# Attention, then four experts: the product of a first-batch pair in six parts, each behind a step's scores

## The chip, the cores and the metric

The kernel runs on one core of one Trainium2 chip. The metric is the device time of one execution in microseconds (us), lower is better: 772.12 us is the median of three runs of the kernel before (770.01 to 773.18).

## The reference

Two batches of eight heads, 768 tokens, 64 dimensions each. Each head's attention is masked by a hash: a query sees a key only where the signs of six projections agree. The attention output, 1536 rows of 512, then runs through four experts of one hidden layer (512 to 1024 to 512), weighted by row.

```python
q_bits = (np.einsum('bhsd,dk->bhsk', q, proj) > 0).astype(np.int64)
k_bits = (np.einsum('bhsd,dk->bhsk', k, proj) > 0).astype(np.int64)
...
mask = q_bucket[:, :, :, None] == k_bucket[:, :, None, :]
scores = scale * np.matmul(q, k.transpose(0, 1, 3, 2))
scores = np.where(mask, scores, -1000000000.0)
scores = scores - np.max(scores, axis=-1, keepdims=True)
attn = np.exp(scores)
attn = attn / (np.sum(attn, axis=-1, keepdims=True) + 1e-09)
return np.matmul(attn, v).astype(np.float32)
...
for e in range(E):
    h = np.maximum(x @ w1[e], 0.0)
    out += p[:, e:e + 1] * (h @ w2[e])
```

## The kernel before

The work comes in three stages. First the attention of batch 0 runs by itself. Then the experts work on batch 0 while the attention of batch 1 is fed in between their matmul groups at a set pace. Last the experts work on batch 1, with fewer products (`moe_fast`).

The attention advances in steps. Step i is query tile t = i mod 6 of head i div 6, so batch 0 has steps 0 to 47 and batch 1 steps 48 to 95; below, "scores 18" are those of step 18. The string `ORDER` says in which order a step's stages are issued, and each stage has a lag, the number of steps by which it trails the scores that it works on:

- S, `stage_s`: four matmuls on TensorE into a score tile `sps`, then a row minimum on VectorE (L368) into the tile `p`. `sps` has the PSUM tag `big`, of which there are two; `tps` and `hps`, used to prepare the next head, take the same two.
- E, `stage_e`: the exponential on ScalarE, one step behind. X, `stage_x`: a transpose on VectorE into `pt` (L415), two steps behind in batch 0, three in batch 1. `pt` has few buffers, so a head's first transpose waits for the product of an earlier pair.
- N, `stage_n`: the reciprocal of a head's row sums, stored to DRAM as `row`. R, `stage_r`: `row` read back from DRAM, spread over 64 partitions, into half of `rdb`.
- V, `stage_v`: the product of the probabilities of a pair of heads with `v` (tiles `tv`, output `pv`), 192 small matmuls in the program. Each of these is two weight loads and two matmuls in the trace, so a pair has 384 there. In batch 0 `pv` lies in four one-bank tiles; in batch 1 it takes both `big` tiles.
- U, `stage_u`: ScalarE copies `pv` out into `xf`, and SP issues the loads of the next pair's `v`. M, `stage_m`: GpSimd scales `xf` by `rdb` and splits it into two parts `xs` (three instructions for each half of the tokens, L465, L467, L470).
- P: one piece of the preparation of the next head (`prep_head`): six transposes `tps` at t = 0, a split on ScalarE and VectorE with copies on GpSimd (`q`, `q`, `k`), then six matmuls `hps` and a copy `ah`, signs on ScalarE, and at last the copies `al` (L332) and `k` on GpSimd. The next head's first scores read `al` and `k`.

A pair's last step is called its end: 11, 23, 35, 47 in batch 0. Before, V of the first three pairs comes in two halves of 96 matmuls, first thing in steps end+3 and end+4; the last pair's comes whole in step 50, and each pair of batch 1 has it whole in step end+4. U follows in step end+5 (51 for the last pair, end+4 in batch 1), M in the next two steps (51 for the last pair). Each engine does its instructions in the order in which they were issued, and so does each queue of DMA issues (SP's above all).

The expert weights are split into two parts on ScalarE and GpSimd (`w1lo`, `w2lo`, L571), the first expert's during the attention of batch 0. The first expert begins when both halves of the last pair are out (`done_b`): 12 matmuls of its first layer (L670 to L672, three for each pair of heads) for each of four blocks of the hidden layer. A group of matmuls of either layer is the unit between which the attention of batch 1 is fed.

Of the kernel before, what the change touches and what calls it, by code (L numbers as in the profile page):

```python
# [8 lines left out]
F32 = mybir.dt.float32  # L9
# [5 lines left out]
P = 128  # L15
# [6 lines left out]
LAG_N = 3  # L22
LAG_R = 4
LAG_X = (2, 3)
LAG_V = (3, 4)
V_PARTS = 2
PV_COST = 1950
# [11 lines left out]
ORDER = "VUXSRMENP"  # L39
# [5 lines left out]
def tile_lsh_attention__then__domain_moe(  # L45
# [24 lines left out]
    GN = S // G  # L70
    NBK = S // 32
# [133 lines left out]
    def load_v(b, h):  # L205
        t = ld.tile([P, QD, NT, D], F32, tag="tv", name="tv", bufs=2)
        for a in range(QD):
            nc.sync.dma_start(
                out=t[a * 32 : (a + 1) * 32], in_=v[b, h].rearrange("(r k c) d -> k r c d", r=QD, c=NT)
            )  # L210
        vvs[b, h] = t
# [179 lines left out]
    def stage_n(b, h):  # L391
# [6 lines left out]
    def stage_r(b, h):  # L398
        j, odd = divmod(h, 2)
        if not odd:  # L400
            rdbs[b, j] = xs.tile([P, S], F32, tag="rdb", name="rdb", bufs=1)
        row = rows.pop((b, h))
        nc.sync.dma_start(
            out=rdbs[b, j][odd * D : (odd + 1) * D], in_=row.rearrange("p t -> (p t)").partition_broadcast(D)
        )
# [11 lines left out]
    def parts_of(b, h):  # L417
        return 1 if b or h >= PB else V_PARTS

    def stage_v(b, j, part, n_parts):  # L420
        if part == 0:
# [4 lines left out]
        n = NBK // n_parts  # L426
        for k in range(part * n, (part + 1) * n):
# [13 lines left out]
    def stage_u(b, j):  # L441
        banks = pvs.pop((b, j))
        for i in range(2):
            vvs.pop((b, 2 * j + i))
            pts.pop((b, 2 * j + i))
            nxt = b * H + 2 * j + 2 + i
            if nxt < len(hseq):
                load_v(*hseq[nxt])
# [6 lines left out]
        for a in range(QD):  # L455
            nc.scalar.activation(xv[:, a], banks[a][:, : NT * 32].rearrange("p (t q) -> p t q", q=32), ACTF.Copy)

    def stage_m(b, h, g):
        j = h // 2
        sl = slice(g * GN, (g + 1) * GN)  # L460
        x = xraw[:, j, sl] if b else xf[j][:, sl]
        tg = NT // G
        rdb = rdbs[b, j].rearrange("d (p t) -> d t p", t=NT)[:, g * tg : (g + 1) * tg]
        x3 = x.rearrange("d (t p) -> d t p", t=tg)
# [8 lines left out]
        if (h, g) == (H - 1, G - 1):  # L473
            done_b[b] = True
# [3 lines left out]
    done_b = [False] * B  # L478

    def attention():  # L480
        n = len(seq)
        prep = [iter(())]

        def do(op, i):
            if op == "N":
                j = i - LAG_N
                if 0 <= j < n and j % NT == NT - 1:
                    stage_n(*seq[j][:2])
            elif op == "R":
                j = i - LAG_R  # L490
                if 0 <= j < n and j % NT == NT - 1:
                    stage_r(*seq[j][:2])
# [14 lines left out]
            elif op in "VUM":  # L507
                for back in range(min(LAG_V), max(LAG_V) + V_PARTS + 3):
                    j = i - back
                    if not 0 <= j < n or j % NT != NT - 1 or seq[j][1] % 2 == 0:  # L510
                        continue
                    b, h, _ = seq[j]
                    part, parts = back - LAG_V[b], parts_of(b, h)
                    if op == "V" and 0 <= part < parts:
                        stage_v(b, h // 2, part, parts)
                        return 2 * PV_COST * b
                    if op == "U" and part == (0 if b else parts):
                        stage_u(b, h // 2)
                    for g in range(G if op == "M" else 0):
                        if part == (parts if (b, h) == (0, H - 1) else (1 if b else 1 + parts) + g):  # L520
                            stage_m(b, h, g)
# [431 lines left out]
```

## Time and profile before

| | |
|---|---|
| time, median of three runs | 772.12 us (770.01 to 773.18) |
| the profiled execution: time, span | 772.6 us, 770.9 us |
| TensorE matmuls busy, share of the span | 720.2 us, 93% |
| VectorE busy | 473.2 us, 61% |
| ScalarE busy | 276.8 us, 36% |
| GpSimd (POOL) busy | 303.9 us, 39% |
| granted TensorE clock, mean | 0.947 |

The profile comes from one execution. "Busy" is time in which an engine has an instruction in work; for TensorE matmuls overlap, and their ends are modelled. PE is TensorE, DVE VectorE, ACT ScalarE, POOL GpSimd, SP the engine whose queue issues nearly all DMAs. [...]

### The profile page before, as it was taken

Reading aid. Unit: us, or ns where it says so; the run is one execution under the profiler, and the core shown is the slowest. Engines: PE = TensorE matmul, PEld = TensorE weight load, DVE = VectorE, ACT = ScalarE, POOL = GpSimd, SP = SyncE. Lnnn points to the kernel's source line nnn. Section 1 sums busy time; section 2 is a strip of 40 time slices with the busy share of each in tenths; the row PEclk is TensorE's granted clock in tenths of the full one; section 3 lists DMA queues with packets and bytes.
Section 4 is the critical chain, followed back from the end, with each engine's and each line's share of the span. In section 5 each row is a group of like instructions: output and inputs, shape, how many; then the busy total and the mean of one; then the engine's idle time right before and its main releaser. Section 6 shows DMA issues by size and latency. Waiting matters only on the chain.

```text
span 770.9 us, 14888 instructions
## 1 busy us (share of the span) xinstructions
PE 720.2 (93%) x6232; PEld 643.3 (83%) x6232; DVE 473.2 (61%) x766; ACT 276.8 (36%) x542; POOL 303.9 (39%) x279
## 2 busy tenths in 40 slices
PE   7888888939989998999899999999999999999998
PEld 5676676839879997899889898989989899899896
DVE  6857667415824781578168233488686686866853
ACT  5646555305303340243133111245343353343430
POOL 5265646132413542453242133375342342433420
PEclk9587887759999999999999999999999999999999
DMA  9335527160215331621422111214131212211202
GB/s 189 63 84 118 115 61 142 33 112 1 58 58 120 79 83 30 147 63 53 121 82 67 30 60 61 82 53 140 56 99 41 79 55 82 82 55 56 84 26 83
DMA packets 65555, 59.76 MB, mean 78 GB/s; under 512 B 38224, under 2 KB 46672, under 8 KB 65488
## 3 DMA queue, kind: packets, MB, share of 16 engines
q1 hardware_dynamic: 64464, 58.48, 30.0%
q8 instruction: 49, 0.80, 0.4%
q10 hardware_dynamic: 1024, 0.33, 0.2%
q14 instruction: 18, 0.15, 0.1%
HBM read 55.60 MB, written 3.19 MB: 76 GB/s over the span
## 4 chain that ended last, share of the span: by engine, by line
PE 87%; DVE 8%; issue 2%; DMA 2%; ACT 0%; POOL 0%; ACTq 0%; SPq 0%; POOLq 0%; DVEq 0%
PE mps L610 11%; PE mps L612 11%; PE mps L611 11%; PE pv L432 10%; PE mps L671 6%; PE mps L670 6%; PE mps L672 6%; PE sps L361 4%; DVE p L368 4%; PE sps L363 4%; DVE pt L415 3%; PE hps L316 3%; PE mps L825 2%; PE mps L821 2%; PE mps L824 2%
## 5 line engine op out<-in xcount | busy, mean ns | idle before, releaser
L610 PE MATMUL mps<-w2hi,hb 128*128 128x512 f32 (+1 forms) x388 | 150.8, 389 | 0.0
L612 PE MATMUL mps<-w2hi,hb 128*128 128x512 f32 (+1 forms) x388 | 150.6, 388 | 0.0
L611 PE MATMUL mps<-w2lo,hb 128*128 128x512 f32 (+1 forms) x388 | 150.4, 388 | 0.0
L384 ACT ACTIVATE p<-p,nb 128x768 f32<-128x768 f32 x96 | 89.8, 936 | 83.3 <-DVE p L368 82.9
L604 DVE SCALAR_TENSOR_TENSOR acc<-mps,pe,acc 128x512 f32<-128x512 f32 (+1 forms) x85 | 63.0, 742 | 86.3 <-PE mps L612 86.2
L368 DVE TENSOR_SCALAR_CACHE_REDUCE p<-sps 128x768 f32<-128x768 f32 x96 | 89.0, 927 | 43.5 <-PE sps L363 43.5
L676 ACT ACTIVATE hb<-mps 128x384 fp32r<-128x384 f32 x64 | 31.4, 490 | 200.8 <-PE mps L672 200.8
L670 PE MATMUL mps<-xs,w1hi 128*128 128x384 f32 x256 | 87.2, 341 | 12.9 <-POOL xs L467 12.3
L677 DVE SCALAR_TENSOR_TENSOR hb<-mps,hb 128x384 fp32r<-128x384 f32 x64 | 35.6, 556 | 95.6 <-ACT hb L676 95.4
L415 DVE STREAM_TRANSPOSE pt<-p 128x768 f32<-128x768 f32 x96 | 92.6, 965 | 0.0
L671 PE MATMUL mps<-xs,w1hi 128*128 128x384 f32 x256 | 87.0, 340 | 0.4 <-POOL xs L470 0.4
L672 PE MATMUL mps<-xs,w1lo 128*128 128x384 f32 x256 | 86.9, 339 | 0.0
L612 PEld LDWEIGHTS mps<-w2hi,hb 128*128 128x128 f32 x388 | 72.8, 188 | 16.1
L611 PEld LDWEIGHTS mps<-w2lo,hb 128*128 128x128 f32 x388 | 72.9, 188 | 14.0
L610 PEld LDWEIGHTS mps<-w2hi,hb 128*128 128x128 f32 x388 | 72.9, 188 | 13.8 <-issue 0.6
L432 PE MATMUL pv<-pt,tv 32*64 32x192 f32 x3072 | 74.5, 342 | 8.4 <-issue 8.4
L807 POOL TENSOR_TENSOR w2lo<-ws,w2hi 128x512 fp32r<-128x512 f32 x32 | 40.6, 1289 | 105.6 <-ACT w2hi L806 105.6
L571 POOL TENSOR_TENSOR w1lo<-ws,w1hi 128x512 fp32r<-128x512 f32 x32 | 41.3, 1291 | 101.7 <-DVE w1hi L579 87.0
L432 PEld LDWEIGHTS pv<-pt,tv 32*64 32x64 f32 x3072 | 66.0, 140 | 16.5 <-issue 14.8
L361 PE MATMUL sps<-ah,q 128*128 128x384 f32 x192 | 60.7, 401 | 17.8 <-DVE p L368 16.6
L571 POOL TENSOR_TENSOR w2lo<-ws,w2hi 128x512 fp32r<-128x512 f32 x32 | 41.3, 1293 | 61.1 <-issue 26.0
L361 PEld LDWEIGHTS sps<-ah,q 128*128 128x128 f32 x192 | 37.1, 216 | 33.5 <-DVE p L368 18.1
(127 smaller groups left out, 1264.2 us busy)
## 6 DMA issues: line engine op xcount, KB each, us to landing
ws<-in_moe_w_dram SPq DMA_DIRECT2D x64, 512.0 KB, 3.7
tv<-in_v_dram SPq DMA_DIRECT2D x64, 192.0 KB, 5.8
rdb<-row SPq DMA_DIRECT2D x16, 192.0 KB, 3.9
out_dram<-acc SPq DMA_DIRECT2D x11, 256.0 KB, 2.1
tqk<-in_q_dram SPq DMA_DIRECT2D x10, 192.0 KB, 6.0
tqk<-in_k_dram SPq DMA_DIRECT2D x10, 192.0 KB, 5.9
tqk<-in_q_dram SPq DMA_DIRECT2D x12, 96.0 KB, 2.9
tqk<-in_k_dram SPq DMA_DIRECT2D x10, 96.0 KB, 3.2
```

What stands on the lines that cost most here:

```text
L361: nc.tensor.matmul(ps[:, i, :NH], q1[:, sl], k1[:, i * NH : (i + 1) * NH], start=True, stop=False)
L368: nc.vector.tensor_scalar(out=two(pt), in0=ps[:, :, :NH], scalar1=MASKED, scalar2=MASKED, op0=ALU.min, op1=ALU.min, accum_out=nb,)
L384: nc.scalar.activation(pt, pt, ACTF.Exp, bias=nb, scale=-1.0, accum_out=den[:, t : t + 1])
L415: nc.vector.transpose(out=pts[b, h][:, :, t], in_=p.rearrange("p (k n) -> p k n", n=32))
L432: nc.tensor.matmul(pvs[b, j][a][i * D : (i + 1) * D, : NT * 32], vvs[b, 2 * j + i][rows, r, c], pts[b, 2 * j + i][rows, k].rearrange("p t ...
L571: nc.gpsimd.tensor_tensor(out=lo[:, c - 1], in0=st[c - 1], in1=hi[:, c - 1].bitcast(F32), op=ALU.subtract)
L610: nc.tensor.matmul(ps, hh[:, ts], w2hi[:, f, cs], start=n == 0, stop=False)
L611: nc.tensor.matmul(ps, hh[:, ts], w2lo[:, f, cs], start=False, stop=False)
L612: nc.tensor.matmul(ps, hl[:, ts], w2hi[:, f, cs], start=False, stop=n == FC - 1)
L670: nc.tensor.matmul(ps[:, :SB], w1hi[:, kk, fs], xhi[b, kk][:, sl], start=kk == 0, stop=False)
L671: nc.tensor.matmul(ps[:, :SB], w1hi[:, kk, fs], xlo[b, kk][:, sl], start=False, stop=False)
L672: nc.tensor.matmul(ps[:, :SB], w1lo[:, kk, fs], xhi[b, kk][:, sl], start=False, stop=kk == KD - 1)
```

## The change

A pair of batch 0 gets its product in six parts of 32 matmuls, in steps end+3 to end+8, each issued behind that step's scores; the last pair has two parts in each of the steps 50, 51 and 52. U comes a step after the last part (end+9, for the last pair 53), M in the two steps after (for the last pair 53 and 54). In batch 1 the product comes in three parts of 64 matmuls in step end+3, behind the scores, with a charge to the pace after each (the pace decides how many expert groups stand between two parts). The reciprocals N come ahead of the scores and a step earlier in batch 0; the rows R of both heads are read in step end+3, ahead of the scores and of v's loads. The `v` of pairs 1 and 3 of batch 0 is loaded into the memory of the output sums, so that a pair's `v` is loaded one pair earlier. The first expert begins its first half of the tokens when that half of the last pair is out (`done_g`), and its second half when the other is.

```diff
-LAG_N = 3
-LAG_R = 4
+LAG_N = (2, 3)
 LAG_X = (2, 3)
-LAG_V = (3, 4)
-V_PARTS = 2
-PV_COST = 1950
+V_AT = (3, 4, 5, 6, 7, 8)
+V_LAST = (3, 3, 4, 4, 5, 5)
+V_LATE = 3
+PV_COST = 3900
...
-ORDER = "VUXSRMENP"
+ORDER = "UXNRSVvwWMEP"
...
     def load_v(b, h):
-        t = ld.tile([P, QD, NT, D], F32, tag="tv", name="tv", bufs=2)
+        shape = [P, QD, NT, D]
+        if (b, h // 2) in ((0, 1), (0, 3)):
+            t = ap_.tile(shape, F32, tag=f"acc{h % 2}", name="tv")
+        else:
+            t = ld.tile(shape, F32, tag="tv", name="tv", bufs=2)
...
-    def stage_n(b, h):
+    def stage_n(b, h, t):
+        if t != NT - 1:
+            return
...
-    def stage_r(b, h):
-        j, odd = divmod(h, 2)
-        if not odd:
-            rdbs[b, j] = xs.tile([P, S], F32, tag="rdb", name="rdb", bufs=1)
-        row = rows.pop((b, h))
-        nc.sync.dma_start(
-            out=rdbs[b, j][odd * D : (odd + 1) * D], in_=row.rearrange("p t -> (p t)").partition_broadcast(D)
-        )
+    def stage_r(b, j):
+        rdbs[b, j] = xs.tile([P, S], F32, tag="rdb", name="rdb", bufs=1)
+        for i in range(2):
+            nc.sync.dma_start(
+                out=rdbs[b, j][i * D : (i + 1) * D],
+                in_=rows.pop((b, 2 * j + i)).rearrange("p t -> (p t)").partition_broadcast(D),
+            )
...
-    def parts_of(b, h):
-        return 1 if b or h >= PB else V_PARTS
-
-    def stage_v(b, j, part, n_parts):
-        if part == 0:
+    def stage_v(b, j, blocks):
+        if blocks.start == 0:
             if b:
                 pvs[b, j] = [x[:, i] for x in (big("pv"), big("pv")) for i in range(2)]
             else:
                 pvs[b, j] = [one("pv") for _ in range(QD)]
-        n = NBK // n_parts
-        for k in range(part * n, (part + 1) * n):
+        for k in blocks:
...
     def stage_u(b, j):
-        banks = pvs.pop((b, j))
-        for i in range(2):
-            vvs.pop((b, 2 * j + i))
-            pts.pop((b, 2 * j + i))
-            nxt = b * H + 2 * j + 2 + i
-            if nxt < len(hseq):
-                load_v(*hseq[nxt])
...
+        for a, bank in enumerate(pvs.pop((b, j))):
+            nc.scalar.activation(xv[:, a], bank[:, : NT * 32].rearrange("p (t q) -> p t q", q=32), ACTF.Copy)
+        for i in range(2):
+            vvs.pop((b, 2 * j + i))
+            pts.pop((b, 2 * j + i))
+            nxt = b * H + 2 * j + i + (2 if b else 4)
+            if nxt < len(hseq) and (b, j) != (0, H // 2 - 1):
+                load_v(*hseq[nxt])
...
+        if (b, j) == (0, H // 2 - 1):
+            done_g[g] = True
...
+    events = {}
+
+    def plan():
+        def at(step, op, f, *args):
+            events.setdefault((step, op), []).append((f, args))
+
+        for b in range(B):
+            for j in range(H // 2):
+                end = (b * H + 2 * j + 1) * NT + NT - 1
+                at(end + 3, "R", stage_r, b, j)
+                if b:
+                    steps, ops = (V_LATE,) * 3, "Vvw"
+                else:
+                    steps, ops = (V_LAST if j == H // 2 - 1 else V_AT), "VVVVVV"
+                n = NBK // len(steps)
+                for part, (step, op) in enumerate(zip(steps, ops)):
+                    at(end + step, op, stage_v, b, j, range(part * n, (part + 1) * n))
+                done = steps[-1] + (not b)
+                at(end + done, "W" if b else "U", stage_u, b, j)
+                for g in range(G):
+                    soon = (b, j) == (0, H // 2 - 1)
+                    at(end + done + (g if soon else 1 + g), "M", stage_m, b, j, g)
...
         def do(op, i):
             if op == "N":
-                j = i - LAG_N
-                if 0 <= j < n and j % NT == NT - 1:
-                    stage_n(*seq[j][:2])
-            elif op == "R":
-                j = i - LAG_R
-                if 0 <= j < n and j % NT == NT - 1:
-                    stage_r(*seq[j][:2])
+                for b, lag in enumerate(LAG_N):
+                    j = i - lag
+                    if 0 <= j < n and seq[j][0] == b:
+                        stage_n(*seq[j])
...
-            elif op in "VUM":
-                for back in range(min(LAG_V), max(LAG_V) + V_PARTS + 3):
-                    j = i - back
-                    if not 0 <= j < n or j % NT != NT - 1 or seq[j][1] % 2 == 0:
-                        continue
-                    b, h, _ = seq[j]
-                    part, parts = back - LAG_V[b], parts_of(b, h)
-                    if op == "V" and 0 <= part < parts:
-                        stage_v(b, h // 2, part, parts)
-                        return 2 * PV_COST * b
-                    if op == "U" and part == (0 if b else parts):
-                        stage_u(b, h // 2)
-                    for g in range(G if op == "M" else 0):
-                        if part == (parts if (b, h) == (0, H - 1) else (1 if b else 1 + parts) + g):
-                            stage_m(b, h, g)
+            elif op in "RVvwUWM":
+                c = None
+                for f, args in events.get((i, op), ()):
+                    f(*args)
+                    if op in "Vvw" and args[0]:
+                        c = 2 * PV_COST // 3
+                return c
...
-                    if (b, h, t) == (0, 0, 4):
-                        load_v(0, 1)
+                    if b == 0 and h < 2 and t in ((4,), (2, 4))[h]:
+                        load_v(0, (h + t) // 2 + 1 if h else 1)
...
-        for i in range(n + max(LAG_V) + 4):
+        for i in range(n + V_LATE + 2):
...
                 if u == 0:
-                    accs[b, tt] = ap_.tile([P, DM], F32, tag=f"acc{tt}", name="acc")
+                    if t == 0:
+                        group = ap_.tile([P, TS, DM], F32, tag=f"acc{s}", name="acc")
+                    accs[b, tt] = group[:, t]
...
+                while not done_g[s]:
+                    next(att)
...
-        while not done_b[0]:
+        while not done_g[0]:
...
-        n_att = H * (NT * 652 + 1632 + PV_COST) + (max(LAG_V) + 4) * DRAIN
+        n_att = H * (NT * 652 + 1632 + PV_COST) + (V_LATE + 2) * DRAIN
```

Three places show what this does to the engines' orders. The first is GpSimd around steps 18 to 24, in which the head with scores 24 to 29 is prepared; before, its `k` tile is called `k_762`.

```order
L465 TENSOR_TENSOR xf<-xf,rdb 128x384
L467 TENSOR_SCALAR xs_111<-xf 128x384
L470 TENSOR_TENSOR xs_111<-xf,xs_111 128x384
L571 TENSOR_TENSOR w1lo<-ws,w1hi 128x512
L220 TENSOR_SCALAR q_759<-ah 64x768 x2
L220 TENSOR_SCALAR k_762<-ah 64x768
L220 TENSOR_SCALAR ah<-al 64x768
L571 TENSOR_TENSOR w1lo<-ws,w1hi 128x512
L332 TENSOR_SCALAR al<-k_762,bit_mul 44x768
L220 TENSOR_SCALAR k_762<-al 12x768
```

After, the same head's tile is `k_719`. The six instructions of M of the first pair (`xf`, `xs_111`), which stood ahead of the preparation, now stand between its `ah` and its `al`, with a weight split among them.

```order
L225 TENSOR_SCALAR ah<-al 64x768
L464 TENSOR_TENSOR xf<-xf,rdb 128x384
L466 TENSOR_SCALAR xs_111<-xf 128x384
L469 TENSOR_TENSOR xs_111<-xf,xs_111 128x384
L582 TENSOR_TENSOR w1lo<-ws,w1hi 128x512
L464 TENSOR_TENSOR xf<-xf,rdb 128x384
L466 TENSOR_SCALAR xs_111<-xf 128x384
L469 TENSOR_TENSOR xs_111<-xf,xs_111 128x384
L337 TENSOR_SCALAR al<-k_719,bit_mul 44x768
L225 TENSOR_SCALAR k_719<-al 12x768
```

The second place is SP's queue at the end of batch 0. Before, the last pair's second row broadcast `rdb` stands behind the eight loads of `tv`, which are issued when the product is done.

```order
L396 DMA row<-rd 128x6
L403 DMA rdb<-row 64x768
L200 DMA tqk<-in_q_dram 128x6x64
L200 DMA tqk<-in_k_dram 128x6x64
L396 DMA row<-rd 128x6
L208 DMA tv<-in_v_dram 32x4x384 x8
L403 DMA rdb<-row 64x768
L191 DMA tqk<-in_q_dram 32x24x32 x2
```

After, both broadcasts of the last pair stand together with no `tv` load between them and their `row`; the `tv` loads (of batch 1's first pair) stand ahead of that and wait for the third pair only.

```order
L213 DMA tv<-in_v_dram 32x4x384 x8
L403 DMA row<-rd 128x6
L201 DMA tqk<-in_q_dram 128x6x64
L201 DMA tqk<-in_k_dram 128x6x64
L408 DMA rdb<-row 64x768 x2
L192 DMA tqk<-in_q_dram 32x24x32 x2
```

The third place is TensorE where batch 1's first pair has its product. Before, all 192 matmuls stand between groups of an expert (`mps`).

```order
L670 MATMUL mps<-xs_114,w1hi 128x384
L671 MATMUL mps<-xs_114,w1hi 128x384
L672 MATMUL mps<-xs_114,w1lo 128x384
L432 MATMUL pv<-pt,tv 64x192 x192
L670 MATMUL mps<-xs_111,w1hi 128x384
L671 MATMUL mps<-xs_111,w1hi 128x384
L672 MATMUL mps<-xs_111,w1lo 128x384
```

After, the first 64 stand right behind a step's scores, and 36 expert matmuls come before the next 64; the same rows stand for the other pairs but that one or four expert groups lie between scores and product.

```order
L621 MATMUL mps<-w2hi,hb 128x512
L622 MATMUL mps<-w2lo,hb 128x512
L623 MATMUL mps<-w2hi,hb 128x512
L366 MATMUL sps<-ah,q_2037 128x384 x2
L368 MATMUL sps<-k_2040,al 128x384 x2
L434 MATMUL pv<-pt,tv 64x192 x64
L621 MATMUL mps<-w2hi,hb 128x512
L622 MATMUL mps<-w2lo,hb 128x512
L623 MATMUL mps<-w2hi,hb 128x512
```

## Rows read from the trace of the kernel before

**Rows 1.** The page, part 2: the granted clock of TensorE by slices, in tenths.
```profile
PEclk9587887759999999999999999999999999999999
```

**Rows 2.** The waits of the whole span: sum in us, times, longest.
```profile
DVE p L368 <- PE sps L363: 43.5, 18, 10.4
```

**Rows 3.** Timeline 130 to 182 us: start, duration, engine, line, tiles [idle before <- releaser].
```profile
142.93 8.94 PE L432 MATMUL pv<-pt,tv 32*64 32x192 f32 x384
...
151.69 1.00 ACT L456 ACTIVATE xf<-pv 128x192 f32<-128x192 f32 x4 [6.37 <-PE pv L432]
...
154.35 4.04 SPq L208 DMA_DIRECT2D tv<-in_v_dram  x8
...
158.61 0.48 SPq L403 DMA_DIRECT2D rdb<-row  x1
...
165.50 1.18 POOL L465 TENSOR_TENSOR xf<-xf,rdb 128x384 f32<-128x384 f32 x1 [22.17 <-DMA rdb<-row]
...
168.42 0.69 PE L671 MATMUL mps<-xs,w1hi 128*128 128x384 f32 x1 [0.39 <-POOL xs L470]
...
174.02 0.52 PE L672 MATMUL mps<-xs,w1lo 128*128 128x384 f32 x1
...
175.22 0.34 PE L670 MATMUL mps<-xs,w1hi 128*128 128x384 f32 x1
```

**Rows 4.** Timeline 51 to 80 us: scores, a pair's first half, copies on POOL.
```profile
54.32 0.58 PE L361 MATMUL sps<-ah,q 128*128 128x384 f32 x2 [0.86 <-DVE p L368]
...
59.78 1.73 POOL L220 TENSOR_SCALAR q<-ah 64x768 fp32r<-64x768 f32 x2
...
68.18 0.58 PE L361 MATMUL sps<-ah,q 128*128 128x384 f32 x2 [0.87 <-DVE p L368]
...
72.56 5.68 PE L432 MATMUL pv<-pt,tv 32*64 32x192 f32 x192
```

**Rows 5.** Timeline 79 to 110 us: that pair's second half and the scores behind it.
```profile
80.12 4.16 PE L432 MATMUL pv<-pt,tv 32*64 32x192 f32 x192
...
84.21 0.62 PE L361 MATMUL sps<-ah,q 128*128 128x384 f32 x2
...
85.02 0.52 PE L361 MATMUL sps<-ah,q 128*128 128x384 f32 x2
...
88.08 0.58 PE L361 MATMUL sps<-ah,q 128*128 128x384 f32 x2 [0.87 <-DVE p L368]
```

**Rows 6.** Windows: length, busy us (instructions) of PE, PEld, DVE, ACT, POOL, clock, DMA.
```profile
54.00:68.00 14.00, 10.92 (x36) 8.60 (x36) 11.88 (x23) 8.57 (x16) 11.76 (x14) 0.63 0.80 145
```

**Rows 7.** Timeline 205 to 245 us: the product of the second batch's first pair.
```profile
217.69 2.86 PE L432 MATMUL pv<-pt,tv 32*64 32x192 f32 x128
...
221.61 2.86 PE L432 MATMUL pv<-pt,tv 32*64 32x192 f32 x128 [1.06 <-issue]
```

**Rows 8.** The waits of TensorE from 168 to 450 us.
```profile
PE pv L432 <- issue: 8.1, 7, 1.7
```

**Rows 9.** The page, part 5: groups of a step; busy us, mean ns | idle before.
```profile
L384 ACT ACTIVATE p<-p,nb 128x768 f32<-128x768 f32 x96 | 89.8, 936 | 83.3 <-DVE p L368 82.9
...
L368 DVE TENSOR_SCALAR_CACHE_REDUCE p<-sps 128x768 f32<-128x768 f32 x96 | 89.0, 927 | 43.5 <-PE sps L363 43.5
...
L415 DVE STREAM_TRANSPOSE pt<-p 128x768 f32<-128x768 f32 x96 | 92.6, 965 | 0.0
```

**Rows 10.** Groups on POOL by shape: busy us, mean ns | idle before.
```profile
L571 POOL TENSOR_TENSOR w1lo<-ws,w1hi 128x512 fp32r<-128x512 f32 x32 | 41.3, 1291 | 101.7 <-DVE w1hi L579 87.0 <-issue 7.6 <-DVE rd L394 5.7
...
L220 POOL TENSOR_SCALAR q<-ah 64x768 fp32r<-64x768 f32 x30 | 27.1, 903 | 62.1 <-ACT ah L229 60.9
...
L465 POOL TENSOR_TENSOR xf<-xf,rdb 128x384 f32<-128x384 f32 x8 | 9.6, 1200 | 30.1 <-DMA rdb<-row 24.2 <-DMA tv<-in_v_dram 4.5 <-ACT xf L456 1.4
L470 POOL TENSOR_TENSOR xs<-xf,xs 128x384 fp32r<-128x384 f32 x8 | 8.0, 1002 | 0.7
...
L467 POOL TENSOR_SCALAR xs<-xf 128x384 fp32r<-128x384 f32 x8 | 4.1, 511 | 0.7
```

More of the change, by code (lines that the diff above doesn't have):

```diff
@@ L70, in tile_lsh_attention__then__domain_moe @@
     GN = S // G
+    TG = NT // G
     NBK = S // 32
@@ L454, in stage_u, with stage_m @@
         xv = x.rearrange("p (t a q) -> p a t q", t=NT, q=32)
[L455 to L459, printed above, removed]
+        for a, bank in enumerate(pvs.pop((b, j))):
[6 more added lines that the diff above has]
+                load_v(*hseq[nxt])
+    def stage_m(b, j, g):
         sl = slice(g * GN, (g + 1) * GN)
         x = xraw[:, j, sl] if b else xf[j][:, sl]
-        tg = NT // G
-        rdb = rdbs[b, j].rearrange("d (p t) -> d t p", t=NT)[:, g * tg : (g + 1) * tg]
-        x3 = x.rearrange("d (t p) -> d t p", t=tg)
+        rdb = rdbs[b, j].rearrange("d (p t) -> d t p", t=NT)[:, g * TG : (g + 1) * TG]
+        x3 = x.rearrange("d (t p) -> d t p", t=TG)
         nc.gpsimd.tensor_tensor(out=x3, in0=x3, in1=rdb, op=ALU.mult)
@@ L472, in stage_m @@
             )
-        if (h, g) == (H - 1, G - 1):
-            done_b[b] = True
+        if (b, j) == (0, H // 2 - 1):
+            done_g[g] = True
     hseq = [(b, h) for b in range(B) for h in range(H)]
     seq = [(b, h, t) for b, h in hseq for t in range(NT)]
-    done_b = [False] * B
+    done_g = [False] * G
+    events = {}
[18 more added lines that the diff above has]
+                    at(end + done + (g if soon else 1 + g), "M", stage_m, b, j, g)
     def attention():
@@ L482, in attention @@
         prep = [iter(())]
+        plan()
         def do(op, i):
             if op == "N":
-                j = i - LAG_N
-                if 0 <= j < n and j % NT == NT - 1:
-                    stage_n(*seq[j][:2])
-            elif op == "R":
-                j = i - LAG_R
-                if 0 <= j < n and j % NT == NT - 1:
-                    stage_r(*seq[j][:2])
+                for b, lag in enumerate(LAG_N):
+                    j = i - lag
+                    if 0 <= j < n and seq[j][0] == b:
+                        stage_n(*seq[j])
             elif op == "X":
```

## The prediction

> **What bounds the kernel now.** I read the page first, for its clock row: TensorE has the full clock from about 175 us to the end, and less than that only ahead of it, in the attention of batch 0 and the handover to the experts [rows 1]. TensorE's waits say the same: behind the handover it waits almost only in the products of batch 1, 8.1 us [rows 8]. So there are three places with something to win or lose: the steps of batch 0, the handover, and the four products of batch 1. The rest is TensorE work that the change doesn't touch.
>
> In the steps of batch 0, VectorE paces. A step costs it a row minimum of 0.93 us and a transpose of 0.97 us [rows 9], a little overlapped; only while a half of a product stands in TensorE's queue ahead of the next scores does it wait: 43.5 us in 18 waits over the span [rows 2].
>
> At the handover the reader is to see one queue. The last product runs from 142.93 to 151.87 us and is copied out by 152.7. But the broadcast of the reciprocals leaves SP only at 158.61, behind eight loads of `tv` issued from 154.35 on, which wait for that product. GpSimd's scaling waits for it until 165.50, and the first expert's group, which needs it, ends at 169.1 (168.42 + 0.69) [rows 3].
>
> **The change, part by part.** I take each term against the profiled execution, 772.6 us, which lies 0.5 us above the median of the runs.
>
> *The handover.* The `tv` loads stand ahead of the last pair's reciprocals now and wait for the third pair alone, so the broadcast lands during the product. What is late next is the product itself, which now has three steps' scores in it, then the chain behind it. Scores of a step cost TensorE 0.81 us at the full clock (84.21 to 85.02) [rows 5]. A product's fixed cost: 192 records take 4.16 us and 128 take 2.86 [rows 5, 7], so 20.3 ns each and 0.26 us for the ends. The product ends at 142.93 + 8.94 + 3 x 0.81 + 2 x 0.26 = 154.8. VectorE is held there: the first transpose of batch 1 needs a `pt` tile that this product reads, and row minimum 51 stands behind it. So from 154.8 on: transpose and minimum, 1.9 us [rows 9], scores 53; another pair, 1.9, scores 54. ScalarE has exponential 51 ahead of the copies, so these end at about 154.8 + 1.9 + 1.1 + 1.0 = 158.8, with 0.94 us and its sum's readout for the exponential [rows 9] and 1.0 for the copies [rows 3]. GpSimd needs 1.20 + 0.51 + 1.00 us [rows 10]: 161.5, and the group ends 0.4 later, at 162. That is 7 us sooner. Three more steps' scores stand ahead of it than before (five, not two): 2.4 us of work done. And before, TensorE was at the low clock behind its wait until about 174.5, with 0.52 us for a matmul that takes 0.34 later [rows 3]: 6 us at up to double price, 2.1 by the ratio and 3.0 by the clock; I take 2.6. Sum 12. Whether the clock holds through the two new waits of 2 us no row says; if not, most of the 2.6 is lost again. I take 11, bounds 7 and 13.
>
> *The products of batch 1.* The first stops after exactly 128 records of matmuls, with as many weight loads, for 1.06 us, and nothing in the profile releases it [rows 7]. All such gaps sum to 8.1 us [rows 8]. [...] I take the gaps as gone: -8.1. New costs: the ends of eight more parts, 8 x 0.26 = 2.1. And the first pair's first third stands right behind a step's scores; it needs both `big` tiles, one of them just scored, freed by VectorE after a transpose and the minimum, 1.9 us, behind whatever output sum is still ahead of them: I take 2.2 us, once, since elsewhere at least one expert group lies between. Net -3.8, I say -4; bounds 0 (gaps half back, or the wait in each pair) and -8.1.
>
> [...]
>
> *Six parts in batch 0.* A pair's twelve steps fall into two halves.
>
> In the first (scores 24 to 30 for the second pair), before: 68.18 to 88.08, 19.9 us, with both halves of the product in it, 5.68 us from a low clock and 4.16 at the full one [rows 4, 5]. VectorE stood still in most of that. After, four of the six parts are there, each 64 records: 0.26 + 64 x 0.0203 = 1.56 us. TensorE then is the engine that paces: scores and part, 2.37 us a step, against 1.9 of VectorE. Up to scores 26, transposes and split of the next head keep the old chain, 4.4 us to the old product's start plus up to 2 us, as scores 26 need the tile that the split still reads: 5.0 to 6.4. Then 4 parts (6.24), 4 scores (3.24), the six `hps` matmuls (about 1.2, as six of scores). Sum 15.7 at the full clock; with a low clock at the start, which cost the old first half 1.5 us (5.68 against 4.16) and would cost scores the same way, about 19. I take 17: -2.9 for a pair, -8.7 for three; bounds -2.4 and -12.6.
>
> In the second half (scores 18 to 24) GpSimd decides. Before: 54.32 to 68.18, 13.86 us, with copies of the next head from 59.78, 5.46 us after scores 18 [rows 4]. GpSimd was busy for 11.76 of these 14 us already [rows 6]; but its six instructions of M were over when the copies began. After, M stands between the head's `ah` and `al`, and scores 24 need `al` and `k`. The chain from the first copy: three copies 2.7, a weight split 1.3 or the wait for `hps` of about as much, `ah` 0.9, M 2 x (1.20 + 0.51 + 1.00) = 5.4, a split 1.3, `al` and `k` 1.8 [rows 10]: 13.4 us. It starts 4.0 to 5.5 us after scores 18 (a part now stands ahead of the transposes, partly where they waited for VectorE, and the clock is higher). The second matmul pair of scores 24 can go at 17.4 to 18.9, the first pair 0.4 sooner; so 17.0 to 18.5 against 13.86: +3.1 to +4.6, I take +3.6. TensorE and VectorE both stand still at the end of it. This holds for the heads scored from 24 and 36 on, twice: +7.2. For the last head of batch 0 M comes after `al`, no term. Net of both halves -1.5, bounds +6.8 and -15, where the last is without the collision, which then saves about 1 us a time.
>
> *Costed at nothing:* the reciprocals' place (0.2 us on VectorE either way), the rows' place in batch 0, since GpSimd gets to M later than they land; the eight loads of `v` that come earlier, hidden behind scores of heads 1 and 2 (if they pushed the next head's loads, some 4 us, as eight took at the handover [rows 3]); the grouped output sums, whose last readers are long done.
>
> Sum: 11 + 4 + 1.5 = 16.5. 772.6 - 16.5 = 756.1, less the 0.5 between this execution and the median: **756 us**.
>
> **The rivals.** *GpSimd doesn't bind* (17 in 100): its chain starts early enough or its idle time swallows M. For it: VectorE paced these steps before. Against it: it was busy for 84% there, and order puts M in the way. Then batch 0 gives 12 instead of 1.5: 745.
>
> *The gaps in batch 1 stay* (10 in 100), because they are not a matter of how long the run of small matmuls is. The term is +4.3 instead of -4: 764. For it: one of the products, the last of batch 0, ran its 384 records in 8.94 us [rows 3], where 0.26 + 384 x 0.0203 = 8.1 is the least, so the length alone does not make them.
>
> *The handover doesn't move* (4 in 100): the broadcast lands early, but the chain behind the product is longer than I have it and eats the gain, down to 2: 765.
>
> *Slower: the clock* (6 in 100). Only a half of 96 matmuls in one go brought the clock up before: 5.68 us from low, then 4.16; in 54 to 68 us, with scores alone, it was 0.63 [rows 4 to 6]. If parts of 1.56 us with stops between don't bring it up, a part costs up to 1.3 us more and its scores up to 0.8. Five of six parts in three pairs (the first is at a low clock in the sum already): 15 x 2.1 = 31, of which GpSimd's chain hides some 5; 756 + 26 = 782. It decides where about 8 of 15 parts run low; then all is lost. [...] Against it: these steps have TensorE busier than VectorE, 2.37 to 1.9.
>
> **How the numbers follow.** My forecast has 63 in 100. The range, 743 to 765 us, takes in its own (748 to 764 from the bounds of the terms, not all at one end), most of the first rival and half of the second; it leaves out the clock and the far ends. A measurement of this kernel can tell about 0.5% from no change. Faster by more than that: forecast and the first three rivals but for their ends, 0.91; within it 0.03; slower 0.06.
>
> **What would show it.** Right: the broadcast `rdb` of the last pair issued before its product ends, the wait of GpSimd for it gone, the first expert's group done by about 155 to 163 us less what batch 0 gains; no stops of 1 us in batch 1's parts; TensorE waiting for a GpSimd copy `k` ahead of scores 24 and 36, for 3 to 5 us. Wrong: that wait missing (the first rival), a clock of 0.5 to 0.7 through the parts (the last), stops that stay in the thirds, or waits of TensorE for VectorE of more than 2 us ahead of each first third.

## The result, and the profile after

The changed kernel takes 763.2 us (median of 4 runs, 762.6 to 764.7) beside 772.5 us (770.0 to 773.2) for the kernel before on the same chip: 0.9888 of the time, with a 95% interval of 0.9862 to 0.9915. It is faster, by 9.3 us and not by the forecast 16.5. Its profiled execution took 764.7 us, 1.5 above its median, so where two traces are set against each other the gain is 7.9 us. The medians here are of fast executions; one of 2417 us, the profiled one of e3 below, is left out.

Some points of the program are common to both traces: the scores of a step, the first matmul of the first expert's second layer, the first matmul with `w1lo` of batch 1's experts. At the second of them the number of steps whose scores are done differs, and a step's scores take 0.69 us among expert matmuls (177.56 to 178.25 us in the changed kernel), so each step more that is done counts as 0.69. "Handover" is the stretch from scores 48 to the second layer, "batch 1" the one from there to batch 1's experts, both corrected by that to the 57 steps of the kernel before.

| start of, us | before | after |
|---|---|---|
| scores 12 / 18 | 32.6 / 54.3 | 32.0 / 50.7 |
| scores 24 / 30 | 68.2 / 88.1 | 62.5 (stopped till 69.0) / 87.2 |
| scores 36 / 42 | 101.9 / 121.9 | 99.7 (stopped till 104.3) / 122.2 |
| scores 48 | 135.4 | 135.8 |
| second layer (steps done) | 191.6 (57) | 187.4 (62) |
| batch 1's experts | 519.0 | 511.1 |
| **handover, corrected** | **56.2** | **51.6 - 3.45 = 48.15** |
| **batch 1, corrected** | **327.4** | **323.7 + 3.45 = 327.15** |

So at scores 48 nothing is won (+0.4), the handover gives 8.05, batch 1 gives 0.25, and behind it both kernels take 251.9 us.

**The steps of batch 0.** The clock row of the page's part 2, which answers to [rows 1]; the slices are 19 us long, and as before all low ones lie in the first ten, up to the handover:

```profile
PEclk9587869789999999999999999999999999999999
```

Timeline of TensorE in a first half (start, duration, engine, line, operation, tiles, [idle before it, and what ended it]):

```profile
75.34 2.86 PE L434 MATMUL pv<-pt,tv 32*64 32x192 f32 x64
...
80.99 1.56 PE L434 MATMUL pv<-pt,tv 32*64 32x192 f32 x64
82.47 0.61 PE L366 MATMUL sps<-ah,q 128*128 128x384 f32 x2
...
83.37 1.56 PE L434 MATMUL pv<-pt,tv 32*64 32x192 f32 x64
```

The reader is to see the first part at the low clock (2.86 us for 64 records), the later ones in 1.56, the figure of the prediction, with 2.38 from part to part. The granted clock, a share of full speed, is 0.50 from 70 to 80 us and 0.99 from 80 to 90. Of the fifteen later parts of the three pairs one took 1.71, all others 1.56. Timeline of the second half in front of it, GpSimd (POOL) and the scores that wait:

```profile
59.16 0.83 POOL L225 TENSOR_SCALAR ah<-al 64x768 fp32r<-64x768 f32 x1
60.07 1.21 POOL L464 TENSOR_TENSOR xf<-xf,rdb 128x384 f32<-128x384 f32 x1
...
66.02 0.99 POOL L469 TENSOR_TENSOR xs<-xf,xs 128x384 fp32r<-128x384 f32 x1
67.12 0.91 POOL L337 TENSOR_SCALAR al<-k,bit_mul 44x768 fp32r<-44x768 f32 x1
68.11 0.83 POOL L225 TENSOR_SCALAR k<-al 12x768 fp32r<-12x768 f32 x1
...
68.99 1.01 PE L368 MATMUL sps<-k,al 76*128 76x384 f32 x2 [5.90 <-POOL k L225]
```

M (lines 464 to 469) stands from 60.07 to 67.0 between `ah` and `al`, and TensorE waits 5.9 us for the `k` behind it. VectorE stands still with it. Its wait for scores over the whole span falls from the 43.5 us of [rows 2] to 32.8, but 10.4 of these 10.7 us are the long wait at the handover, which is there again under another name, as its transpose's wait for the product (10.81 below). In the steps themselves, 12 to 142 us, it is 32.6 before and 30.4 after, so the parts' gain is nearly eaten up. The view of waits, whole span (sum, times, longest), VectorE's row and two of TensorE's:

```profile
DVE p L373 <- PE sps L368: 32.8, 27, 5.0
```

```profile
PE sps L368 <- POOL k L225: 9.5, 2, 5.9
PE pv L434 <- DVE pt L421: 2.1, 1, 2.1
```

**The handover**, same timeline, 143 to 162 us, beside [rows 3]:

```profile
143.80 1.23 SPq L408 DMA_DIRECT2D rdb<-row  x2
...
144.60 3.04 PE L434 MATMUL pv<-pt,tv 32*64 32x192 f32 x128
...
152.84 0.62 PE L368 MATMUL sps<-k,al 76*128 76x384 f32 x2 [0.97 <-issue]
153.39 3.44 PE L434 MATMUL pv<-pt,tv 32*64 32x192 f32 x128
156.48 0.98 DVE L421 STREAM_TRANSPOSE pt<-p 128x768 f32<-128x768 f32 x1 [10.81 <-PE pv L434]
...
158.47 0.77 PE L366 MATMUL sps<-ah,q 128*128 128x384 f32 x2 [1.64 <-DVE p L373]
...
160.54 1.22 POOL L464 TENSOR_TENSOR xf<-xf,rdb 128x384 f32<-128x384 f32 x1 [14.17 <-ACT xf L451]
...
161.63 0.52 PE L685 MATMUL mps<-xs,w1hi 128*128 128x384 f32 x1
...
163.41 1.20 POOL L464 TENSOR_TENSOR xf<-xf,rdb 128x384 f32<-128x384 f32 x1
...
165.15 0.52 PE L687 MATMUL mps<-xs,w1lo 128*128 128x384 f32 x1
```

The broadcast leaves before the product begins, and GpSimd waits for ScalarE's copy alone. But the product ends at 156.5, TensorE then has nothing to do but wait for VectorE's chain, and the first group, 161.63 to 165.7, runs at the low clock: 0.52 us for a matmul, one every 0.32. From 158.4 to 165.4 us the granted clock is 0.52; in the kernel before it is 0.50 from 157.7 to 174.7, of which TensorE waits up to 167.3, so it works at the low clock about as long. GpSimd begins the second half of the tokens at 163.41. So the first half was done before the group's last three matmuls, which need it, and no wait stands there: what binds is TensorE's own queue.

**Batch 1.** The first pair's first third, beside [rows 7]:

```profile
192.88 0.51 PE L366 MATMUL sps<-ah,q 128*128 128x384 f32 x2
...
193.68 0.53 PE L434 MATMUL pv<-pt,tv 32*64 32x192 f32 x2
196.32 4.92 PE L434 MATMUL pv<-pt,tv 32*64 32x192 f32 x126 [2.10 <-DVE pt L421]
201.17 0.50 PE L621 MATMUL mps<-w2hi,hb 128*128 128x512 f32 x1
```

No stop of 1 us is left anywhere in batch 1 [rows 8], but this third stands right behind scores and a transpose, waits 2.1 us for the latter, and then runs at the low clock, 4.92 us where 128 records take 2.86 (granted clock 0.57 from 196 to 200 us, 1.00 ahead of it). From its start to the next matmul it takes 7.49 us. The first thirds of the second and third pair wait too, though expert matmuls lie between them and the scores: 4.26 and 3.51 us, where the other nine thirds take 2.78 or 2.79. The third pair's:

```profile
354.40 0.55 PE L434 MATMUL pv<-pt,tv 32*64 32x192 f32 x8
355.15 2.83 PE L434 MATMUL pv<-pt,tv 32*64 32x192 f32 x120 [0.19 <-DVE p L373]
357.91 0.45 PE L685 MATMUL mps<-xs,w1hi 128*128 128x384 f32 x1
```

### The profile page after: what moved, and what is told of

Read it like the earlier page. It is cut to its first block, busy times and chain, and to the rows that moved or that the text cites. A ratio compares the mean times of both kernels' runs of the same rounds, so it can differ in the third digit from the quotient of the medians.

```text
span 763.0 us, 14891 instructions
## 1 busy us (share of the span) xinstructions
PE 723.2 (95%) x6232; PEld 636.7 (83%) x6232; DVE 471.7 (62%) x766; ACT 276.3 (36%) x542; POOL 303.8 (40%) x279
## 4 chain that ended last, share of the span: by engine, by line
PE 86%; DVE 7%; POOL 3%; issue 2%; ACT 1%; DMA 0%; ACTq 0%; DVEq 0%; POOLq 0%
PE mps L621 11%; PE mps L623 11%; PE mps L622 11%; PE pv L434 10%; PE mps L685 6%; PE mps L687 5%; PE mps L686 5%; PE sps L366 4%; PE sps L368 4%; PE hps L321 2%; DVE pt L421 2%; DVE p L373 2%; PE mps L840 2%; PE mps L836 2%; PE mps L839 2%
## 5 line engine op out<-in xcount | busy, mean ns | idle before, releaser
L373 DVE TENSOR_SCALAR_CACHE_REDUCE p<-sps 128x768 f32<-128x768 f32 x96 | 89.3, 930 | 32.9 <-PE sps L368 32.8
L434 PE MATMUL pv<-pt,tv 32*64 32x192 f32 x3072 | 79.8, 343 | 2.8 <-DVE pt L421 2.1
L434 PEld LDWEIGHTS pv<-pt,tv 32*64 32x64 f32 x3072 | 63.9, 139 | 15.9 <-issue 9.6
L366 PE MATMUL sps<-ah,q 128*128 128x384 f32 x192 | 59.8, 396 | 17.2 <-DVE p L373 14.9
L368 PE MATMUL sps<-k,al 76*128 76x384 f32 x192 | 56.6, 379 | 10.6 <-POOL k L225 9.5
```

Of the source, the lines that this page charges most:

```text
L366: nc.tensor.matmul(ps[:, i, :NH], q1[:, sl], k1[:, i * NH : (i + 1) * NH], start=True, stop=False)
L368: nc.tensor.matmul(ps[:, i, :NH], q2[0:MQE, sl], k2[0:MQE, i * NH : (i + 1) * NH], start=False, stop=True)
L373: nc.vector.tensor_scalar(out=two(pt), in0=ps[:, :, :NH], scalar1=MASKED, scalar2=MASKED, op0=ALU.min, op1=ALU.min, accum_out=nb,)
L434: nc.tensor.matmul(pvs[b, j][a][i * D : (i + 1) * D, : NT * 32], vvs[b, 2 * j + i][rows, r, c], pts[b, 2 * j + i][rows, k].rearrange("p t ...
```

## The experiments

Each was timed beside the kernel before on the same chip; e11 is a single execution. e1 to e4 ran on one chip, e5 to e8 on a second, e9 and e10 on a third, and the kernel before took 773.5, 773.9 and 772.4 us there, so differences in us across these groups are good to about 1.5. A ratio is to the kernel before. The changed kernel, run once more as a base (e5), gave 764.2, 0.9874 (0.9850 to 0.9898).

> The changed kernel once more, as the base for the runs beside it: 0.9888 of the kernel before, as measured, so 763 to 765.

**e1: M behind the last copies.**

```diff
-at(end + done + (g if soon else 1 + g), "M", stage_m, b, j, g)
+at(end + done + (g if soon else 1 + g if b else 3 + g), "M", stage_m, b, j, g)
```

> The changed kernel with GpSimd's M for the first three pairs of batch 0 two steps later, behind the head's last copies `al` and `k` and not between them. Theory (M's place makes TensorE wait for `k`): the 9.5 us of waits for `k` ahead of scores 24 and 36 go, the second halves lose their 7 us, 763 becomes 756 to 758; scores 18 to 24 take about 14 us again. Rival (GpSimd has too much work in these steps wherever M stands): M then delays the next head's copies by its 5.4 us, the first halves grow by what the second ones lose, 762 to 764.

754.5 us, 0.9767 (0.9741 to 0.9793), 9.7 below e5 (8.3 by the ratios). Timeline of its scores 24 and GpSimd:

```profile
61.27 0.91 POOL L337 TENSOR_SCALAR al<-k,bit_mul 44x768 fp32r<-44x768 f32 x1
62.26 0.83 POOL L225 TENSOR_SCALAR k<-al 12x768 fp32r<-12x768 f32 x1
...
63.14 1.01 PE L368 MATMUL sps<-k,al 76*128 76x384 f32 x2 [0.19 <-POOL k L225]
63.17 1.20 POOL L464 TENSOR_TENSOR xf<-xf,rdb 128x384 f32<-128x384 f32 x1
```

The wait is 0.19 and M follows, in a stretch where nothing waits for it: scores 24 to 30 take 18.8 us (62.3 to 81.1) beside 18.6 for 12 to 18, where no M stands; 30 to 36 take 11.9, and scores 48 come at 125.8, 10.0 sooner. M's place is the cause; the rival falls. The gain is larger than expected since second halves without the wait are shorter than before (11.8 and 11.9 against 13.9 and 13.8); VectorE's wait for scores in the steps is down to 20.2 us (12 to 132).

**e2 and e6: the handover alone, in the kernel before.** e2 moves the rows ahead of the loads of `v`, e6 the reciprocals too:

```diff
-ORDER = "VUXSRMENP"
+ORDER = "VRUXSMENP"    # e2
+ORDER = "VNRUXSMEP"    # e6
```

> The kernel before with one edit: the broadcast of the reciprocals issued ahead of the loads of `v`, all products as they were. Theory A (the handover alone is worth 12 or more, and the changed kernel lost 4 of it again by putting scores into the last product): TensorE's wait of 12.3 us ahead of the first group goes, and with it some of 2.6 us at the low clock: 758 to 761. Rival B (the handover is worth what the changed kernel's trace shows, 8 us, however the product is cut): 764.5. Rival C (a wait behind it takes its place): 769 to 772.

766.5 us, 0.9922 (0.9898 to 0.9946): 7.0 us, near B in size. The mechanism is C's, as its timeline shows:

```profile
152.99 0.96 DVE L368 TENSOR_SCALAR_CACHE_REDUCE p<-sps 128x768 f32<-128x768 f32 x1 [10.63 <-PE sps L363]
...
153.87 0.19 DVE L394 RECIPROCAL rd<-den 128x6 f32<-128x6 f32 x1
...
156.07 0.48 SPq L403 DMA_DIRECT2D rdb<-row  x1
...
159.55 1.19 POOL L465 TENSOR_TENSOR xf<-xf,rdb 128x384 f32<-128x384 f32 x1 [16.29 <-DMA rdb<-row]
```

The reciprocal itself is late: on VectorE it stands behind row minimum 50, whose scores stand behind the product. So a shorter wait took the first one's place (6.1 us of TensorE ahead of the first group, where it was 12.3), and e6 was made to take both away.

> The kernel before with the reciprocals ahead of a step's scores and the broadcast ahead of the loads of `v`; all products as they were. Theory (with the rows alone ahead, the reciprocal stood on VectorE behind a row minimum that waits for the product, so the broadcast still came late; both moves together free GpSimd): TensorE's wait for GpSimd ahead of the first group, 12.3 us in the kernel before and 6.1 with the rows alone, goes, and some of the low clock behind it: 757 to 760. Rival (the reciprocal's place is worth the 0.2 us that the prediction gave it): 766, as with the rows alone.

756.7 us, 0.9780 (0.9753 to 0.9808): 17.2 us, from two letters of an order.

```profile
141.46 0.19 DVE L394 RECIPROCAL rd<-den 128x6 f32<-128x6 f32 x1
...
143.53 0.48 SPq L403 DMA_DIRECT2D rdb<-row  x1
...
151.99 1.23 POOL L465 TENSOR_TENSOR xf<-xf,rdb 128x384 f32<-128x384 f32 x1 [9.54 <-ACT xf L456]
...
152.47 0.34 PE L670 MATMUL mps<-xs,w1hi 128*128 128x384 f32 x1
```

The first group runs right behind the product and two steps' scores, at the full clock (0.34). The corrected handover is 134.5 to 175.3 = 40.8 us, 15.4 less than before; the changed kernel, with the same two moves in it, has 48.15.

**e3 and e11: the last product of batch 0 in one part.**

```diff
-V_LAST = (3, 3, 4, 4, 5, 5)
+V_LAST = (3,)
```

> The changed kernel with the last product of batch 0 in one part again, behind scores 50. Theory A (each part's scores push the product's end, and VectorE, ScalarE's copies and GpSimd behind it): the product ends 3 us sooner, the copies stand ahead of exponential 51 again, GpSimd is done 6 us sooner, two scores fewer stand ahead of it (1.6): 758 to 760. Rival B (scores in it cost nothing): 762.5 to 764.

With the number of parts the copies U and the scaling M of that pair move too, two steps forward (from 53 to 51), and the first expert with them.

756.2 us, 0.9787 (0.9763 to 0.9812), 8 us below e5 (6.7 by the ratios) and more than A has; B falls. e11 is the same kernel once more, for its trace.

> The kernel of e3 once more, for its trace: where the 7.8 us that it saves against the changed kernel lie. Theory A, as for e3 (all at the handover): the first product of a second layer starts 7 to 8 us sooner than in the changed kernel, scores counted, and the rest takes as long. Theory B (from the traces of e1 and e7): 3 to 4 us there, and 4 in batch 1, where the first pair's thirds no longer wait for a transpose right behind a step's scores.

It took 757.1 us. Timeline of its handover:

```profile
149.06 2.86 PE L434 MATMUL pv<-pt,tv 32*64 32x192 f32 x128 [0.38 <-issue]
...
153.06 2.84 PE L434 MATMUL pv<-pt,tv 32*64 32x192 f32 x122 [1.14 <-issue]
155.74 1.00 ACT L451 ACTIVATE xf<-pv 128x192 f32<-128x192 f32 x4 [9.67 <-PE pv L434]
...
156.64 0.34 PE L685 MATMUL mps<-xs,w1hi 128*128 128x384 f32 x1
...
158.74 0.44 PE L685 MATMUL mps<-xs,w1hi 128*128 128x384 f32 x1 [0.18 <-POOL xs L466]
```

The product ends hardly sooner (155.7), but the copies no longer stand behind exponential 51, so GpSimd begins at 156.88 and not at 160.54; scores and the group's first matmuls are still there to fill TensorE's wait for it, and the clock stays up (0.34 for a matmul; the page's clock row has a 9 for 151 to 170 us). Whether the product in one part wins this, or the copies that come two steps sooner with it, this edit does not part. Corrected, the handover is 181.6 - 136.4 - 2 x 0.69 = 43.8 us, 4.3 less than in the changed kernel, and batch 1 is 503.4 - 181.6 + 1.4 = 323.2, 4.0 less. Theory B holds: other steps meet other expert groups, and its view of waits for batch 1 has 0.5 us for a transpose where the changed kernel has 2.1. The traces of e7 and e9 below, also with 59 steps done at the second layer, have 323.3 and 323.2 us for batch 1; that of e1, with 62, has 327.5. Which step meets which group, no edit here set by itself.

**e4 and e8: batch 1's thirds.** e4 makes the products whole again, in the new place behind the scores.

```diff
-steps, ops = (V_LATE,) * 3, "Vvw"
+steps, ops = (V_LATE,), "V"
...
-c = 2 * PV_COST // 3
+c = 2 * PV_COST
```

> The changed kernel with the four products of batch 1 in one part each again. Reading of the trace (gaps of 8.1 us are gone, but the ends of the parts, waits behind a step's scores and a first part at a low clock give it all back): 762.5 to 764, no difference. Rival (the prediction's term): 4 us more, 767.

771.0 us, 0.9977 (0.9957 to 0.9996), 7 us above the changed kernel: my reading was wrong, and the prediction's own term nearer. View of waits of TensorE, 185 to 460 us:

```profile
PE pv L434 <- issue: 5.5, 7, 1.7
PE pv L434 <- DVE pt L421: 2.1, 1, 2.1
```

The stops are back, beside the new wait. Corrected, batch 1 takes 515.0 - 185.1 + 3.45 = 333.35 us, 6.2 more than with thirds and 5.95 more than whole products had in the old place. So with products in this place the cut wins about 6, and for whole products the place behind the scores loses about 6. The other way to show it is to leave the thirds and move them back, one step later and ahead of transposes and scores; e7's kernel is the base, as its edits were known to win.

```diff
-V_LATE = 3
+V_LATE = 4
...
-ORDER = "UXNRSVvwWMEP"
+ORDER = "ZYyUXNRSVWMEP"
...
-steps, ops = (V_LATE,) * 3, "Vvw"
+steps, ops = (V_LATE,) * 3, "ZYy"
...
```

> As e7, and the thirds of batch 1's products stand one step later at the start of a step, ahead of the transposes and scores, as the whole products did in the kernel before. Theory (thirds win 4 us by the gaps, and standing right behind a step's scores and transposes costs 4 by waits and a low clock): 3 to 4 us below e7. Rival (what costs is the ends of the parts, which stay): within 1 us of e7.

741.7 us, 0.9595 (0.9572 to 0.9619), 4.3 below e7. In the traces batch 1 takes 486.0 - 167.9 = 318.1 us against 492.9 - 171.0 = 321.9, both with 59 steps done: 3.8 less. All that TensorE waited for from 165 to 460 us:

```profile
PE sps L366 <- ACT xraw L451: 1.0, 1, 1.0
PE hps L321 <- DVE al L235: 0.2, 1, 0.2
```

Neither stops nor transposes: corrected 319.5, which is 7.9 below the kernel before, nearly all of its 8.1 us of stops [rows 8].

**e7: the edits of e1 and e3 together.**

> The changed kernel with two edits together: M of the first three pairs behind the last copies, and the last product of batch 0 in one part. If what they save is apart (a wait for `k` in the steps, a longer product at the handover): 0.988 x 0.990 of the changed kernel, 746 to 748. If both win the same thing, the full clock at the handover: 751 to 754.

746.0 us, 0.9641 (0.9618 to 0.9664). That is 18.3 below e5, where e1 and e3 alone are 9.7 and 8.0 below it (by the ratios 18.0 against 8.3 and 6.7): they add up, and the rival falls. Its trace has both, scores 48 at 125.4 us and a corrected handover of 44.3.

**e9: two halves in place of six parts**, on e7's kernel, with M ahead of the next head's copies:

```diff
-V_AT = (3, 4, 5, 6, 7, 8)
+V_AT = (3, 4)
```

> As e7, but the first three products of batch 0 in two halves, each behind a step's scores, and M at once behind them, ahead of the next head's copies (so no wait for `k` either). Theory (six parts let VectorE work on between them, where a half stops it): the steps of batch 0 take what they took in the kernel before, scores 48 come 8 to 9 us later than in e7: 754 to 755. Rival (what wins is that the product stands behind the scores and not ahead, whatever the number of parts): within 2 us of e7, 746 to 748.

762.1 us, 0.9868 (0.9846 to 0.9890), 16 above e7 and outside both ranges. Scores 48 come at 139.2 in place of 125.4, and TensorE has no wait for `k` ahead of them. Timeline of its second pair:

```profile
82.65 4.16 PE L434 MATMUL pv<-pt,tv 32*64 32x192 f32 x192
82.76 0.96 DVE L373 TENSOR_SCALAR_CACHE_REDUCE p<-sps 128x768 f32<-128x768 f32 x1 [6.22 <-PE sps L368]
...
87.74 0.96 DVE L373 TENSOR_SCALAR_CACHE_REDUCE p<-sps 128x768 f32<-128x768 f32 x1 [3.13 <-PE sps L368]
```

VectorE stops behind each half. The parts do it, not the place behind the scores; why scores 48 come 4 us later than in the kernel before (135.4) stays open.

**e10: e8, with the last product ahead of scores 50** (an operation of its own, `F`, at the front of the order).

```diff
-ORDER = "ZYyUXNRSVWMEP"
+ORDER = "FZYyUXNRSVWMEP"
```

> As e8, and the last product of batch 0 ahead of scores 50, not behind them, as in the kernel before. Theory (ahead of them it ends 0.8 us sooner, and the scores fill TensorE's wait for the copies and GpSimd behind it): 1 to 3 us below e8, 739 to 741. Rival (the first group comes sooner by 0.8 but has a step's scores more behind it): as e8, 741 to 742.

741.5 us, 0.9602 (0.9581 to 0.9624): no difference to e8. In its trace the corrected handover is 171.0 - 126.9 - 1.4 = 42.7 us against e8's 43.7, 1 us, which these intervals cannot tell; the time is nearer the rival's. e6's handover, 40.8, is still shorter, and 1.4 us of that is a stop in e10's product that e6's does not have. e8 and e10 beat both kernels, the one before by 31 to 32 us.

## Why the prediction came out as it did

The signs and most mechanisms were right, and the time lay inside the range; the forecast was 7 us too low. The range held by its width: the three terms that were to win came out 9.4 us short together, all on one side. Its terms against the two traces:

| term | predicted | measured | by |
|---|---|---|---|
| handover | -11 | -8.05 | traces; e6, e11 |
| batch 1 | -4 | -0.25 | traces; e4, e8 |
| first halves | -8.7 | -6.0 | traces |
| second halves | +7.2 | +7.0 | traces; e1 |
| ahead of scores 12 | 0 | -0.6 | traces |
| sum | -16.5 | -7.9 | |

**Handover.** The step "so the broadcast lands during the product" was right, with the issue at 143.80. Two sizes failed, and the path. "I take 2.6" for the low clock was not saved: the prediction said that no row tells whether the clock holds through two new waits, and it did not hold. The second group of matmuls runs at the full clock now, but the first, of which nine had run at it before (0.34), runs at the low one: about 7 us of work at the low clock in either kernel. And the product ended at 156.5, not 154.8: it began after scores 50 at the low clock, its parts took 3.04, 2.86 and 3.44, and 0.97 went in a stop. The prediction's path behind it, copies and GpSimd, did not bind: the whole first group stands behind scores 53 and 54 in TensorE's queue, which wait for VectorE, and it ended at 165.7 in place of 162. Before it had ended at 169.4, not at 169.1, as its last matmul stands behind the row that the prediction took. e6 and e11 point to what was missed: work for TensorE that stands behind the product fills its wait for the copies, and with the scores in the product and the group two steps later it is gone. e6 shows it with the product whole; that the parts alone cost it in the changed kernel is argued, not shown. That "the reciprocals' place" was costed at nothing was wrong in what it stood on: e2 against e6 shows it worth 10 us, the difference of 7.0 and 17.2. In my sum it did no harm, since I had both moves together in one term.

**Batch 1.** "I take the gaps as gone" was right, and so the rival that they stay (764) is refuted though the time came close to it. The step that failed is the wait of the first pair, "I take 2.2 us, once": it was 2.1 us, but the low clock behind it cost 2.1 more (4.92 against 2.86), and it came more than once. Against 2.79 for a third without a wait, the first thirds of the first three pairs lost 4.7, 1.5 and 0.7 us, 6.9 in all, and TensorE's wait for ScalarE's copies `xraw` was 2.0 against 1.0. 8.1 - 6.9 - 1.0 leaves 0.2, what was measured. The parts' ends, 2.1 in the sum, look smaller in net, as e8 gets 7.9 of 8.1 back.

What makes the stops, and so why a third should have none, no run shows. What the runs show is where they stood: stops of 0.38 and 1.14 us 128 matmuls with 128 loads apart in e11's product, 8.1 us of them in batch 1 before [rows 8], 5.5 us with e4's whole products, and none in the thirds of the changed kernel and of e8.

**First halves.** I had 15.7 at the full clock and about 19 with a low clock at the start, and took 17. They took 18.7, 18.6 and 18.3, and in e1 18.6, 18.8 and 19.0: the low clock is there each time (first part 2.86, scores of 1.01). The rows showed this case (5.68 for a half) and I took the middle of two. That cost 1.3 to 1.7 us a pair; the term is off by only 2.7 since the first pair's first half was 21.7 before, where I had counted 19.9 for all, which is luck. The 15.7 itself stands on the low end of its own 5.0 to 6.4, and it was about right: in e8's trace the second pair stays at the full clock (first part 1.56, a 9 in the page's clock row for 55 to 92 us) and takes 16.0 (62.6 to 78.6), where e7's, with the same program up to there, takes 18.5. So both cases occur, and an execution can fall into either.

**Second halves.** Right, to the place: M between `ah` and `al`, TensorE waiting for `k` ahead of scores 24 (5.90) and 36 (3.62), and the halves 4.0 and 2.9 us longer for 3.6 each (each taken up to the stop's end less 0.4, the time of the stopped scores' first two matmuls). The rival that GpSimd does not bind is refuted by these; e1 is what it would have looked like, with 9.6 us won in batch 0 up to scores 48 where the rival had 12.

**The clock in the parts.** The slower rival is refuted: from the second part on 14 of 15 take 1.56 us, at a granted clock of 0.99 from 80 to 90 us. That only a half of 96 matmuls had brought it up was wrong: in the trace before it is 0.55 from 54 to 65.5 us and 1.00 from 65.5 to 72.3, with transposes, scores and `hps` alone in both stretches. In the changed kernel's parts, with no wait of TensorE from a pair's second to its sixth, the clock did not fall back: it is 1.00 from 42.7 to 66.5, from 80.3 to 97.2 and from 114.4 to 134.8 us, where the later parts of the three pairs lie. At the handover, where TensorE waited 1.64 and 0.34 us ahead of the first group, it fell once (0.52 from 158.4 to 165.4 us) and rose again (1.00 from 165.6 to 190).

**The rival that the handover doesn't move** is refuted, by 8.05.

## What to carry to other kernels

When a transfer that came late is moved up, look at once for what is late next on the way to it: the row's reciprocal stood behind the same product as its transfer, and one move without the other was worth 7 of 17 us. Small pieces of a long product were worth much where another engine is paced by what stands between them (six parts in place of two halves: 746.0 us against 762.1), but the last one was better whole here, with work left behind it to fill TensorE's wait (43.8 us of handover against 48.15), so cut the first three and leave the last whole. Work that is put later must be checked on every engine that it lands on: M's new place on GpSimd took back all that the parts had won.

## What the runs showed of the hardware

Long runs of small matmuls (32x192) stopped for 0.2 to 2.0 us, in some traces at two places 128 of them and their loads apart. In the last product of batch 0 the stops of e8, e9 and e11 stand after 134 and after 262 records (0.52, 0.22 and 0.38 us, then 1.14 in each); e7 has one alone, after 262, of 1.97 us, and the same product in the kernel before ran its 384 with none in its timeline. Thirds of 128 with expert groups between them had none in the changed kernel and in e8. And in batch 1 of the changed kernel the low clock came back where TensorE had waited only about 2 us: after 2.1 us the granted clock was 0.57 from 196 to 200 us, and one third took 4.92 us in place of 2.86. Behind e7's stop of 1.97 us it did not: the next 122 records took 2.84.
